# A new hand-planned order for a fused long-convolution and MLP kernel: GpSimd passes set apart from VectorE's products, diagonals on GpSimd, four row statistics on ScalarE

## The chip, the core and the metric

The kernel runs on one core of a Trainium2 chip. The time is the device time of one execution in microseconds (us); several executions are given by their median. A profile is one further execution recorded by the hardware profiler, with its own time. The engines are TensorE (PE in the profile; its weight loads are the row PEld), VectorE (DVE), ScalarE (ACT), GpSimd (POOL) and SyncE (SP), which here issues all DMAs on one queue.

## The reference, cut to what matters

All arrays are bfloat16; the sequence has 2048 rows, the width D is 512, the MLP's inner width 1792.

```python
x = A_q
h = x + A(layernorm(x), A_k, A_v, A_shift_k, A_ssm_k, A_ssm_D)
h2 = h + B(layernorm(h), B_w1, B_w2, B_w3, B_w4)

def A(q, k, v, shift_k, ssm_k, ssm_D):
    k_shift = sum over t in 0..3 of k_pad[:, t:t + S, :] * shift_k[:, 3 - t]
    kv = k_shift * v
    y = irfft(rfft(kv, 4096) * rfft(ssm_k, 4096))[:S]     # causal convolution per column
    return q * (y + kv * ssm_D)

def B(x, w1, w2, w3, w4):
    h = gelu(layernorm(x) @ w1)
    x1 = x + concat(quarters of h shifted by 1, -1, 2, -2 rows) @ w2
    return x1 + gelu(layernorm(x1) @ w3) @ w4
```

## The kernel before

**Two halves.** The 2048 rows are split in two sets `s` = 0 and 1 of eight blocks `b` of 128 partitions. The convolution is done as a Fourier transform by matmuls, in parts: the filter's first and second half (F0, F1) and the signal kv of either half (A0, A1). The first half needs only A0 with F0; the second needs A0 with F1 and A1 with F0.

**Tasks.** `body` first lists 784 tasks, each with a number, the engines that may do it, a function that issues its instructions, and what it depends on. The kinds that matter here:

- `Lf`, `Lk`, `Lv`, `Lq`, `Lw1` to `Lw4`: loads (L265 to L287, L569 to L572), 256 or 260 KB each, `Lv` 512 KB.
- `dg` (L295 to L310): the diagonal matrices of the four taps for column chunk `c`. On VectorE it is four `tensor_scalar` instructions (L307), on GpSimd one `affine_select` (L299).
- `K`, `KV`: the shift of k by matmuls with those diagonals (L442) and the product with v on VectorE (L450).
- `bits`, `cons`, `ttv`, `tta`, `f2v`, `f2a`, `ftv`, `fta`, then `tts`, `f2s`, `ft` on ScalarE: angle tables and their sines (L312 to L367); `tt`, `f2` (L370 to L378) finish them; `dr` adds ssm_D into the filter (L294).
- `S1`, `E1`, `X`, `S2`, `E2`: one forward transform: matmuls (L389), copy from PSUM (L257, on ScalarE or VectorE), a DMA that turns the layout (L405), matmuls (L413), copy from PSUM (L257; for F1 a folding by VectorE, L425).
- `P`: the products of two spectra, VectorE `tensor_tensor` of 128x2048 (L474), 8 for the first half (`conv(0)`) and 16 for the second; `I2`, `EV`, `XI`, `I1`: the inverse transform (L484, L257, the DMA of L495, L502).
- `Q`, `QV`, `QP`, `QN`: mean and variance of the rows of q: one `bn_stats` for each block on VectorE (L506), their variance for eight blocks at once, the power -0.5 on GpSimd (L529), the scales. `Y` normalizes one block of q into `z_t` (L608 to L613, GpSimd, ScalarE or VectorE); `H` adds the convolution (L616); `HS` and `SS` are statistics of rows (VectorE L602 and L603, or ScalarE L600).
- `uw`, `rr`, `hn`, `hb` and `ux`, `r1`, `xn`, `lb`: the two layer norms of the MLP part, for pairs of blocks (L623 to L649, L736 to L763); `hb` and `lb` write a normalized block (L653, L655).
- `LT`, `TE` and `LX`, `EX`: transposes of such a block, either on TensorE (L670) with a copy (L257), or by DMA through DRAM (L663, L665).
- `W`, `U` (L699, L703), `X2`, `S`, `R` (L722, L725, L729): the first MLP and its residual; `M`, `G` (L777, L781), `O`, `Z`, `OUT` (L790, L792, L794): the second MLP, by pairs of blocks.

**The order.** The string `ORDER` (L31 to L62) holds one word for each task: its number, the letter of the engine that does it (P TensorE, V VectorE, A ScalarE, G GpSimd, S the DMA queue), and digits for the buffers that it takes (`ps` is one of eight PSUM banks). `Plan.emit` (L79) issues the tasks in this order, so that each engine's queue holds its own words in order; between engines there are only the waits for data and for buffers, which the framework adds. The costs (`{V: 0.5, GP: 0.9}`) and the `port` marks in `add` were of use to the planner that wrote the string; nothing reads them when the kernel runs.

## Time and profile before

| | us |
|---|---|
| median of 3 runs (lowest, highest) | 215.55 (214.04, 215.84) |
| the profiled execution's own time | 213.26 |
| its span, first to last instruction | 211.6 |
| first instruction of the first product (L474) starts | 30.43 |
| first sum of the first half (`H`, L616) starts | 49.66 |
| first matmul with w1 (L699) in TensorE's queue | 61.8 |
| last product (L474) ends | 105.67 |
| last write to the output tile (L792) ends | 208.5 |

The granted TensorE clock was 1.00 throughout. In the views that follow, times count from the span's start; "windows" gives each engine's busy time in a stretch; "groups" gives instructions of one line and form with their count, their busy time, and the mean in ns; the timeline merges equal instructions that follow each other and gives in brackets the idle time ahead of them with what ended it.

### The profile page before, as it was taken

To read this page: it belongs to the slowest core of one execution; us is meant where nothing else is said; L and a number is where in the kernel's file an instruction comes from. 1 tells how busy PE (TensorE), PEld (TensorE's weight loads), DVE (VectorE), ACT (ScalarE), POOL (GpSimd) and SP (SyncE) were. 2 spreads that over 40 slices of the span, in tenths; PEclk is the share of its full clock that TensorE was granted. 3 is DMA by queue.
4 is the path that set the end of the run, shared out by engine and by line. 5 is a ranking of instruction groups with operands and counts; after the bars stand their busy time and mean duration, and the time that the engine had idled before them with its cause. 6 is when DMAs were issued, how large, how long until landed. Compare 5 with 4: busy or idle time off the path is not lost.

```text
span 211.6 us, 5040 instructions
## 1 busy us (share of the span) xinstructions
PE 195.7 (93%) x1964; PEld 116.2 (55%) x1980; DVE 144.8 (68%) x302; ACT 125.5 (59%) x206; POOL 80.1 (38%) x177
## 2 busy tenths in 40 slices
PE   6899769898889999979999999989999999999992
PEld 5454323442248546636744884645848888645450
DVE  6998999999999999999868971559972000112031
ACT  3979989787999658943751883364623565301010
POOL 7850059804888140287044683212765000000000
PEclk9999999999999999999999999999999999999999
DMA  6999895976948995000693008533146440010011
GB/s 173 313 403 397 321 325 222 256 205 237 371 169 294 332 435 147 0 28 13 89 232 92 27 22 181 98 69 82 42 107 154 102 74 0 3 50 34 16 50 50
DMA packets 30809, 32.86 MB, mean 155 GB/s; under 512 B 20545, under 2 KB 22594, under 8 KB 30530
## 3 DMA queue, kind: packets, MB, share of 16 engines
q1 hardware_dynamic: 30786, 32.55, 50.8%
q8 instruction: 15, 0.25, 0.5%
q14 instruction: 8, 0.07, 0.1%
HBM read 13.14 MB, written 4.46 MB: 83 GB/s over the span
## 4 chain that ended last, share of the span: by engine, by line
PE 59%; DVE 13%; ACT 12%; DMA 6%; issue 3%; POOL 3%; SPq 3%; DVEq 0%; ACTq 0%; POOLq 0%
PE ps L777 21%; PE ps L790 18%; ACT r_a L257 5%; PE ps L722 5%; PE ps L699 5%; PE ps L484 3%; DVE r_v L616 3%; DMA r_dg<-dhb 2%; DMA r_a<-r_a 2%; PE ps L502 2%; PE ps L413 2%; DMA r_k<-in_kt_dram 2%; DVE r_f L425 2%; DVE r_dg L307 1%; DVE r_p L474 1%
## 5 line engine op out<-in xcount | busy, mean ns | idle before, releaser
L777 PEld LDWEIGHTS <-r_k 128*128 128x128 bf16 x448 | 43.5, 98 | 7.7 <-issue 1.2
L792 DVE TENSOR_TENSOR r_v<-ps,r_v 128x512 bf16<-128x512 f32 x16 | 10.7, 686 | 42.4 <-PE ps L790 42.4
L474 DVE TENSOR_TENSOR r_p<-r_a,r_f 128x2048 bf16<-128x2048 bf16 x24 | 28.7, 1240 | 1.0 <-PE ps L484 0.6
L777 PE MATMUL ps<-r_dg,r_k 128*128 128x256 bf16 x224 | 25.6, 273 | 0.1
L257 ACT CAST r_a<-ps 128x1024 bf16<-128x1024 f32 x23 | 22.2, 1026 | 3.0 <-PE ps L413 2.8
L781 ACT ACTIVATE r_f<-ps 128x512 bf16<-128x512 f32 x14 | 7.8, 599 | 20.6 <-PE ps L777 20.6
L613 POOL TENSOR_SCALAR z_t<-r_q,qrs,qnm 128x512 f32<-128x512 bf16 x11 | 13.0, 1188 | 12.6 <-DVE r_v L616 12.0
L442 PE MATMUL ps<-r_dg,r_k 128*128 128x256 bf16 (+3 forms) x108 | 15.2, 284 | 1.6 <-ACT r_f L257 0.8
L257 ACT CAST r_vs<-ps 128x1024 bf16<-128x1024 f32 x14 | 13.7, 1032 | 4.9 <-PE ps L484 4.9
L725 DVE SCALAR_TENSOR_TENSOR r_q<-r_v,hrr,ps 128x512 bf16<-128x512 bf16 x16 | 11.4, 742 | 5.9 <-PE ps L722 3.7
L781 ACT ACTIVATE r_a<-ps 128x512 bf16<-128x512 f32 x14 | 7.8, 606 | 12.2 <-PE ps L777 12.2
L257 ACT CAST r_f<-ps 128x1024 bf16<-128x1024 f32 x14 | 13.2, 1023 | 3.0 <-PE ps L389 2.8
L442 PEld LDWEIGHTS <-r_k 128*128 128x128 bf16 x112 | 9.5, 98 | 9.5 <-issue 4.8
L484 PE MATMUL ps<-r_p,ttab 32*64 32x512 bf16 x384 | 13.3, 379 | 1.0 <-DVE r_p L474 0.8
L699 PEld LDWEIGHTS <-r_fx 128*128 128x128 bf16 x128 | 12.3, 98 | 3.2 <-DMA r_dg<-dhb 0.6
L600 ACT ACTIVATE junk<-r_v 128x512 bf16<-128x512 bf16 x14 | 8.9, 635 | 7.3 <-DVE r_v L616 7.1
L777 PE MATMUL ps<-xtx,r_k 128*128 128x256 bf16 x112 | 13.0, 273 | 0.0
L600 ACT ACTIVATE junk<-r_q 128x512 bf16<-128x512 bf16 x12 | 7.6, 630 | 9.2 <-DVE r_q L725 9.1
L777 PE MATMUL ps<-xty,r_k 128*128 128x256 bf16 x112 | 12.7, 272 | 0.0
L790 PE MATMUL ps<-w4s,r_f 128*128 128x512 bf16 x54 | 12.5, 379 | 0.1
L748 POOL TENSOR_TENSOR xrr<-xrr,mhalf 128x2 f32<-128x2 f32 x8 | 7.2, 900 | 14.2 <-DVE xrr L745 13.8
L389 PEld LDWEIGHTS <-f 128*32 128x32 bf16 x256 | 6.1, 95 | 11.3 <-issue 7.5
(183 smaller groups left out, 374.7 us busy)
## 6 DMA issues: line engine op xcount, KB each, us to landing
r_z<-r_vs SPq DMA_DIRECT2D x16, 256.0 KB, 3.9
r_k<-in_kt_dram SPq DMA_DIRECT2D x8, 260.0 KB, 4.6
r_v<-in_v_dram SPq DMA_DIRECT2D x4, 512.0 KB, 7.3
r_f<-r_f SPq DMA_DIRECT2D x8, 256.0 KB, 5.2
r_q<-in_q_dram SPq DMA_DIRECT2D x8, 256.0 KB, 5.7
r_a<-r_a SPq DMA_DIRECT2D x8, 256.0 KB, 4.2
r_f<-r_a SPq DMA_DIRECT2D x8, 256.0 KB, 4.2
r_a<-r_z SPq DMA_DIRECT2D x8, 256.0 KB, 4.1
```

The lines of the kernel that those rows point to most:

```text
L257: (act.copy if e in "AM" else on[e].tensor_copy)(o, i)
L442: nc.tensor.matmul(o[:, (d + j0) * P:(d + j1 + 1) * P], lhsT=kT[s][c][:, bb, x:x + P], rhs=diag[:, c, j0:j1 + 1, :].rearrange("p j x -> p ...
L474: on[e].tensor_tensor(out=prs[:, sl[0]:sl[0] + 2, :, :], in0=sp[a][:, kl, :, :, :], in1=gv, op=MUL)
L484: nc.tensor.matmul(ps[64 * t:64 * t + 64, bk[h], :], lhsT=ttab[32 * h:32 * h + 32, 2 * kl + t, 2 if x else xx, :], rhs=prs[32 * h:32 * h + ...
L600: act.activation(junk[:], x, ACT.Square, accum_out=sq[:, i, 1:2])
L613: on[e].tensor_scalar(out=z_t[:, sl[0], :], in0=qs, scalar1=qrs[:, i:i + 1], scalar2=qnm[:, i:i + 1], op0=MUL, op1=ADD)
L699: nc.tensor.matmul(ps[:, sl[0], j * 256:(j + 1) * 256], lhsT=w1s[:, k, m * P:(m + 1) * P], rhs=xt[:, k, :], start=(k == 0), stop=(k == DC ...
L725: vec.scalar_tensor_tensor(out=q_sb[:, s, b, :], in0=h_sb[s][:, b, :], scalar=hrr[:, 4 * s + b // 2, 0, b % 2:b % 2 + 1], in1=ps[:, got((" ...
L777: nc.tensor.matmul(ps[:, sl[0], j * 256:(j + 1) * 256], lhsT=w3s[:, k, fc * P:(fc + 1) * P], rhs=xt[:, k, :], start=(k == 0), stop=(k == D ...
L781: act.activation(gb[:, 2 * fp:2 * fp + 2, :], ps[:, got(("M", s, p, fp))[0], :].rearrange("p (j x) -> p j x", j=2), ACT.Gelu_apprx_tanh)
L790: nc.tensor.matmul(ps[:, sl[0], :], lhsT=gb[:, fc, (b % 2) * P:(b % 2 + 1) * P], rhs=w4s[:, fc, :], start=(fc == 0), stop=(fc == FC - 1))
L792: add(("Z", s, b), {V: 0.61}, lambda e, sl, b=b: vec.tensor_tensor(out=h_sb[s][:, b, :], in0=ps[:, got(("O", s, b))[0], :], in1=h_sb[s][:, ...
```

## The change

The statements are these; the string `ORDER` is replaced as a whole (30 lines), of which the first lines and the last one are shown.

```diff
 ORDER = """
-004S 029P0 000S 002S 003S 005S 008S 031V 037V 001S 030P 063P23 006S 055P45 009S 057P67 064V 007S 056A 038G 065P01 010S 058A 019S 059P45 033V 045G
-061P23 060A 087P60 039G 036V 062A 095P71 046V 042V 066A 093P4 032G 043V 047A 074S 101P5 044A 034G 015S 094V 051P23 022S 088V 053P01 035G 023S 052A
...
-747A 750P0 699S 753P2 751V 752S 754V 755S
+002S 029P0 000S 005S 004S 003S 008S 031V 037V 006S 030P 055P23 021S 057P45 007S 033G 056V 010S 058A 001S 038G 095P10 009S 023S 063P67 042V 059P45 015S
+036G 064A 061P23 022S 034G 101P0 060A 043V 045V 065P67 062A 046V 039V 087P41 019S 047A 044A 097P5 035G 040V 066A 102V 099P2 041A 073S 096V 032G 091P3
...
+699S 781P6 695V 696S 782V 783S
 """
...
     def dg(c):
         def f(e, sl):
-            if e == GP:
-                tap = r_k[:, c * KW + NB * 129:(c + 1) * KW].rearrange("p (j x) -> p j x", x=2)[:, :, 1:2]
-                pool.affine_select(out=diag[:, c], in_=tap.to_broadcast([P, 4, P]), compare_op=OP.is_equal, fill=0.0, base=0,
-                                   pattern=[[0, 4], [-1, P]], channel_multiplier=1)
-                return
-            for j in range(4):
-                sc = r_k[:, c * KW + NB * 129:(c + 1) * KW].rearrange("p (o x) -> p o x", o=1)[:, 0, :].bitcast(F32)[:, j:j + 1]
-                if e == A:
-                    act.activation(diag[:, c, j, :], ident[:], ACT.Copy, scale=sc)
-                else:
-                    vec.tensor_scalar(out=diag[:, c, j, :], in0=ident[:], scalar1=sc, scalar2=None, op0=MUL)
+            tap = r_k[:, c * KW + NB * 129:(c + 1) * KW].rearrange("p (j x) -> p j x", x=2)[:, :, 1:2]
+            pool.affine_select(out=diag[:, c], in_=tap.to_broadcast([P, 4, P]), compare_op=OP.is_equal, fill=0.0, base=0,
+                               pattern=[[0, 4], [-1, P]], channel_multiplier=1)
         return f
     for c in range(DC):
-        add(("dg", c), {V: 0.8, A: 1.19, GP: 0.85}, dg(c), [("Lk", 0, c)], port="VG")
+        add(("dg", c), {GP: 0.65}, dg(c), [("Lk", 0, c)], port="VG")
...
     def qstat(s, b):
-        return lambda e, sl: vec.bn_stats(qst[:, 8 * s + b, :], q_sb[:, s, b, :])
+        if s == 0 or b < 4:
+            return lambda e, sl: vec.bn_stats(qst[:, 8 * s + b, :], q_sb[:, s, b, :])
+
+        def f(e, sl):
+            act.activation(junk[:], q_sb[:, s, b, :], ACT.Identity, accum_out=qst[:, 8 * s + b, 0:1])
+            act.activation(junk[:], q_sb[:, s, b, :], ACT.Square, accum_out=qst[:, 8 * s + b, 1:2])
+        return f
...
+            if s:
+                j = slice(12, 16)
+                en.tensor_scalar(out=qmv[:, j, 0], in0=qst[:, j, 0], scalar1=1.0 / D, scalar2=0.0, op0=MUL, op1=ADD)
+                en.tensor_tensor(out=qrs[:, j], in0=qmv[:, j, 0], in1=qst[:, j, 0], op=MUL)
+                en.tensor_tensor(out=qsd[:, j], in0=qst[:, j, 1], in1=qrs[:, j], op=SUB)
+                i = slice(8, 16)
...
-            add(("Q", s, b), {V: 0.6}, qstat(s, b), [("Lq", s, b // 2)])
+            add(("Q", s, b), {A: 1.3} if s and b > 3 else {V: 0.6}, qstat(s, b), [("Lq", s, b // 2)])
```

The four statistics on ScalarE are those of blocks 4 to 7 of the second half: two activations with an accumulator each, in place of one `bn_stats`. With the new string these tasks change their engine (tasks of one kind, before and after):

| kind | VectorE | ScalarE | GpSimd |
|---|---|---|---|
| dg | 2, 0 | | 2, 4 |
| Q | 16, 12 | 0, 4 | |
| ftv, f2v | 0, 2 | | 2, 0 |
| E1, E2, EV (copies) | 22, 21 | 58, 59 | |
| HS, SS | 6, 9 | 26, 23 | |
| TE, EX (copies) | 5, 5 | 9, 9 | |
| Y | 4, 2 | 1, 3 | 11, 11 |
| hb, lb | 7, 9 | 6, 8 | 19, 15 |
| uw, ux | 7, 8 | | 9, 8 |
| hn, xn | 9, 9 | | 7, 7 |

TensorE's tasks and the DMAs are the same in number and size; their order is new. In the DMA queue the loads of v come later in the front end (`Lv` as tenth and twelfth transfer, before as ninth and eleventh), the loads of q for the first half earlier, and three of the second half's loads (`Lf` 1,0 and 1,1 and `Lk` 1,1), which stood ahead of the last two transfers `X` of A0, come behind them. On TensorE the first down projections `O` (0,3) and `O` (0,2) come ahead of the inverse transform `I2` (1,1), the last `I1` comes behind five of the next up projections, and the second half's last four pairs run in the order 0, 1, 2, 3 (before 1, 2, 0 and 3).

More of the change, by code (lines that the diff above doesn't have):

```diff
@@ new lines @@
+616G 580A 256V 569P7 617G 576A 618G3 513V 573P2 570A 275V01 414A 260P0145 577P6 509V 572A 505V 574A 578A 584P7 261V 621G2 516A 587V 277V23 619P61
+622P3 585V 588G 581P2 620A 623A 586S 589V 497V 262A 590G0 279V45 592S 591G1 281V67 273S 276P01672 278P 287V01 280P 282P 593S 289V23 624P30 284A 630P4
+291V45 283A 286S 626P5 625A 285S 582V 631A 632P6 293V67 288P01230 633A 290P 416A 299V01 292P 294P 301V23 628P4 295A 636P7 303V45 296A 634P6 627A 298S
+305V67 629A 583S 300P01231 637A 297S 302P 410V 635A 322G 304P 412V 306P 418V 638P5 307A 419G 308A 309S 310S 420V 594S2 430V1 641P4 421G3 427V0 501V
```

52 lines of the change are left out of this document (24 added, 28 removed).

## The prediction

> **What bounds the kernel now.** I read the page's busy times first, then windows cut at the milestones of the table above, then groups by form, and last the timeline where engines hand over.
>
> ```profile
> span 211.6 us, 5040 instructions
> PE 195.7 (93%) x1964; PEld 116.2 (55%) x1980; DVE 144.8 (68%) x302; ACT 125.5 (59%) x206; POOL 80.1 (38%) x177
> ```
>
> ```profile
> core 0: us, PE busy (x) PEld busy (x) DVE busy (x) ACT busy (x) POOL busy (x), PEclk, DMA share, GB/s
> 0.00:30.40 30.40, 25.36 (x317) 13.91 (x328) 27.19 (x62) 24.92 (x29) 13.23 (x69) 1.00 0.91 320
> 30.40:49.60 19.20, 16.57 (x272) 6.95 (x261) 18.18 (x18) 16.01 (x17) 10.70 (x8) 1.00 0.80 246
> 49.60:61.80 12.20, 10.87 (x135) 3.42 (x134) 11.81 (x33) 11.25 (x21) 10.03 (x20) 1.00 0.66 247
> 61.80:107.50 45.70, 44.01 (x600) 28.20 (x601) 44.49 (x72) 32.15 (x57) 18.84 (x34) 1.00 0.55 175
> 107.50:158.70 51.20, 50.01 (x332) 30.88 (x324) 36.54 (x110) 26.04 (x55) 24.31 (x43) 1.00 0.41 90
> 158.70:211.60 52.90, 48.92 (x336) 32.86 (x336) 6.61 (x11) 15.17 (x28) 2.97 (x5) 1.00 0.21 53
> ```
>
> The averages hide two kernels. Up to 61.8 us VectorE is nearly never idle (27.19 of 30.40, 18.18 of 19.20, 11.81 of 12.20), the DMA engines are 0.91 busy at first, and TensorE loses 61.8 - 25.36 - 16.57 - 10.87 = 9.0 us outright. From 61.8 on TensorE sets the end: it idles 1.69 and 1.19 us in the next two stretches, and the last one is its own work but for the final sum and output. Its work there is the same after the change. So the time can fall by as much as the front end reaches that point earlier, and by the idle 2.9 us.
>
> **The change, part by part.** The sum is made against the profiled execution, 213.26 us with a span of 211.6; it lies 2.29 below the median of 215.55.
>
> ```profile
> L474 DVE TENSOR_TENSOR r_p<-r_a,r_f 128x2048 bf16<-128x2048 bf16 x24 | 28.7, 1240 | 1.0 <-PE ps L484 0.6
> L257 DVE CAST r_a<-ps 128x1024 bf16<-128x1024 f32 x9 | 10.8, 1214 | 0.4 <-PE ps L389 0.3
> L450 DVE TENSOR_TENSOR r_kv<-ps,r_v 128x512 bf16<-128x512 f32 x16 | 10.2, 679 | 0.0
> L307 DVE TENSOR_SCALAR r_dg<-ident,r_k 128x128 bf16<-128x128 bf16 x8 | 3.1, 466 | 0.5 <-DMA r_k<-in_kt_dram 0.5
> L299 POOL TENSOR_SCALAR_AFFINE_SELECT r_dg<-r_k 128x512 bf16<-128x512 bf16 x2 | 1.3, 636 | 1.8 <-DMA r_k<-in_kt_dram 1.8
> ```
>
> ```profile
> L365 DVE TENSOR_SCALAR r_a<-r_a 128x64 int32<-128x64 int32 x1 | 0.7, 651 | 0.0
> L357 DVE TENSOR_SCALAR r_a<-r_a 128x512 int32<-128x512 int32 x1 | 0.4, 427 | 0.0
> ```
>
> *1, up to the first product (30.43 us).* VectorE loses the eight instructions of L307, 3.1 us together, and one product with v (0.68 with its place behind the first product). It gains the table passes `ftv` and `f2v`: two of 128x512 integers at 0.43 (L357) and two of 128x32, at 0.2 each between nothing and L365's 0.65: 1.3. Net 3.1 + 0.7 - 1.3 = 2.5 off its queue. GpSimd gains two diagonals at 0.64 and loses as much or more; `cons` now waits behind the first diagonal, and so for a load, which puts the tables back by up to that diagonal's 0.64, beside copies on ScalarE that hide it. The transfers are the other limit: of those ahead of the first product's spectrum none goes away, while 3 of 256 or 260 KB leave the queue ahead of A0's last (0.78 MB at the 320 GB/s of the first window: 2.4 us, which counts in step 2). So the gain is from 0 (transfers decide) to 2.5 (VectorE decides). I take 1.7, nearer to VectorE, whose first stretch is 0.89 busy with chains on it besides.
>
> *2, first product to first sum `H` (30.43 to 49.66).* Counted in the two orders, VectorE has one 1.21 copy less and one 0.68 product with v more: -0.5. Its idle 19.20 - 18.18 = 1.0 there is made of short waits for spectra and inverse transforms, all of which start earlier now. GpSimd's `Y` pass hits the products:
>
> ```profile
> L613 POOL TENSOR_SCALAR z_t<-r_q,qrs,qnm x11: 767/773/3726, 34.3 to 115.5; 128x512 f32<-128x512 bf16 x11
> ```
>
> ```profile
> 39.54 2.89 DVE L474 TENSOR_TENSOR r_p<-r_a,r_f 128x2048 bf16<-128x2048 bf16 x2
> ```
>
> One `Y` took 3.73 instead of 0.77, under products back to back; and this pair of products took 2.89 where 2 x 1.24 = 2.48 is usual, 0.4 lost. In the new order all four `Y` are planned behind the eighth product. Gain 0.5 to 1.9; I take 1.2. Floor below nothing: four `Y` that each cost a product 0.4 make it 1.6 less.
>
> *3, first sum to last product (49.66 to 105.67).* Here VectorE is the bound (11.81 + 44.49 of 57.9 busy), so its queue counts. Three `bn_stats` leave this stretch, and hb passes, copies and one resid; statistics of rows, three transposes' copies and norms come in. Counted task by task at the groups' means the two queues differ by 0.1 us: nothing. The other `bn_stats` stood behind the last product, and what hides them is TensorE's two down projections there (it is 1.69 idle in the whole stretch): nothing either, and at most 0.7 if that cover were gone. The three added small operations of `QV` lie in the same place.
>
> *4, TensorE from 61.8 to 107.5.* Two waits go, one comes.
>
> ```profile
> 87.14 1.93 PE L484 MATMUL ps<-r_p,ttab 32*64 32x512 bf16 x64
> 89.01 3.19 PE L790 MATMUL ps<-w4s,r_v 128*128 128x512 bf16 x13
> 92.59 0.40 PE L670 MATMUL ps<-ident,nbx 128*128 128x128 bf16 x4 [0.39 <-ACT nbx L653]
> 93.69 0.40 PE L670 MATMUL ps<-ident,nbx 128*128 128x128 bf16 x4 [0.71 <-POOL nbx L655]
> ```
>
> ```profile
> 86.95 0.64 ACT L600 ACTIVATE junk<-r_q 128x512 bf16<-128x512 bf16 x1
> 87.72 0.63 ACT L600 ACTIVATE junk<-r_q 128x512 bf16<-128x512 bf16 x1
> ```
>
> The transposes `LX` (0,0), (0,1) waited 0.39 and 0.71 for their input; now a down projection of 3 us stands ahead of both: -1.1. But the inverse transform of 1.93 us that stood between the seventh up projection and the first down projection is gone from there, and on ScalarE the statistic of block 4 (two passes, 87.72 - 86.95 = 0.77 apart: 1.5 us) now stands ahead of the last three gelus that the down projection needs. Queued behind that wait: both `LX`, the second down projection, then `I2` (1,1); VectorE's `Z` (0,3) and the products behind it wait with it. I take +1.4; from 0 (ScalarE is ahead) to 3.0 (a second statistic shortly before it counts too).
>
> *5, from 107.5 on.*
>
> ```profile
> L699 PEld LDWEIGHTS <-r_fx 128*128 128x128 bf16 x128 | 12.3, 98 | 3.2 <-DMA r_dg<-dhb 0.6
> ```
>
> ```profile
> 130.83 4.84 DMA r_dg<-dhb
> 135.71 4.49 PE ps L699 x32
> 207.82 0.69 DVE r_v L792
> ```
>
> TensorE idles 1.19 here, 0.6 of it ahead of 135.71 for a transpose by DMA (pair 1 of the second half) that was issued second at 130.83; it is now issued first. Late next is the transpose for pair 2, issued behind six writes: I give back 0.3 and take -0.9 (-1.2 to +1). All later work is TensorE's, instruction for instruction the same, with the same end (`O`, `Z`, `OUT`): nothing.
>
> Sum: -1.7 - 1.2 + 0 + 1.4 - 1.1 - 0.9 = -3.5. Profiled 213.3 becomes 209.8; the median, 215.55 - 3.5 = **212.0 us**. The likeliest case's own range, with the terms' spreads not all to one side, is 209.9 to 214.1.
>
> **Rivals.**
>
> *Transfers decide the front end.* Step 1 gives nothing: -1.8, **213.8**. For it the DMA share of 0.91; against it that VectorE was as busy, and did not wait.
>
> *The change does not keep them apart.* `ORDER` sets each queue's own order; as built, no `Y` of the first half waits for a product, only for its scales, which were ready when the first `Y` began at 34.3, amid products. Where GpSimd gets in between two products, each costs 0.4, four 1.6, and step 2's gain is gone: -3.5 + 1.2 + 0.4 = -1.9, **213.7**. For it the 2.89 above; against it that one `Y` in four did so before.
>
> *Table passes and diagonals collide.* L365, with 64 elements, took 0.65, as long as the diagonal beside it on GpSimd, and L307's 128x128 took 0.47. Three diagonals at 0.64 among the table passes put VectorE's chain back by up to 1.9, part of which the wait for v's load hides; 1.3 of it on the path makes -3.5 + 1.3 = -2.2, **213.4**. [...]
>
> *ScalarE becomes the bound (slower).*
>
> ```profile
> L653 ACT ACTIVATE r_k<-r_v,hnm,hrr 128x512 bf16<-128x512 bf16 x2 | 1.6, 814 | 0.9 <-DVE hnm L641 0.9
> ```
>
> Eight statistics passes (6.2), three more hb (2.4) and two more `Y` (1.6) come to it, one copy more (0.9), while three row statistics and one lb go (3.1): about +8.0 us, much of it in 49.6 to 61.8 where it is already 11.25 of 12.20 busy. Without step 4's wait the change gains 4.9. The kernel is no faster once 4.9 of the 8.0 fall on TensorE's path, slower by over 1% from 7.1; all of it: 215.55 - 4.9 + 8.0 = **218.7**. Against it: 13.5 us of ScalarE are free between 61.8 and 107.5.
>
> *Everything fits.* Steps 1 and 2 at their best, no new wait: -2.5 - 1.9 - 1.1 - 0.9 = -6.4, **209.2**.
>
> **How the numbers follow.** Forecast 0.45; transfers 0.12; not apart 0.10; collisions 0.08; ScalarE 0.17; all fits 0.08. About 1% (2.2 us) is what a measurement can tell from no change. Below 213.4: four fifths of the forecast (0.36), all of the last (0.08), and about 0.4 of the three weak cases (0.12): 0.56. Above 217.7: three quarters of ScalarE (0.13) and 0.07 for several small losses together: 0.20. Within: 0.24. The range takes in every case but the worst of ScalarE: 208.8 to 217.6.
>
> **What would show it.** Step 1: first product near 28.7 instead of 30.43, no L307. Step 2: first `H` near 46.8, no product over 1.3. Step 3: last product near 102.8. Step 4: a TensorE wait of about 1.4 for ScalarE's gelu ahead of the first down projection, none at the first `LX` pair. Step 5: the last four pairs start about 3.5 us earlier. Wrong if the first product stands at 30 or later, if TensorE's waits for ScalarE sum to 3 or more between 60 and 107, or if the tail has idle TensorE.

## The result, and the profile after

The change made the kernel slower. The median is 217.91 us over 21 runs (215.09 to 220.01) against 214.42 us over 21 runs of the kernel before (213.13 to 215.84). The ratio is 1.0105, with a 95% interval from 1.0077 to 1.0132; it leaves out runs over 1.5% above the fastest of their kernel, so it is smaller than the ratio of the medians. In microseconds the loss is 2.3 by the ratio and 3.5 by the medians; the forecast was a gain of 3.5.

The profiled execution after took 217.91 us, as long as its median. These are the head of its page, and its windows cut at the same events as those of before: first product, first sum `H`, the up projection `W` (0,0,0), the start of the two down projections behind the last products, and the end of the third pair of down projections.

```profile
span 215.9 us, 5091 instructions
PE 197.5 (92%) x1964; PEld 115.9 (54%) x1980; DVE 143.8 (67%) x299; ACT 132.8 (62%) x221; POOL 79.2 (37%) x177
...
PEclk9999965899999999999999999999999999999999
```

```profile
0.00:32.10 32.10, 25.65 (x312) 12.91 (x320) 25.73 (x56) 23.63 (x28) 12.61 (x66) 0.95 0.91 314
32.10:54.10 22.00, 19.51 (x285) 7.77 (x282) 17.87 (x18) 18.54 (x20) 12.87 (x10) 0.84 0.70 187
54.10:66.60 12.50, 10.22 (x130) 3.98 (x124) 12.38 (x31) 11.99 (x22) 10.24 (x28) 1.00 0.76 245
66.60:112.20 45.60, 43.39 (x605) 27.27 (x606) 43.49 (x74) 35.98 (x69) 18.60 (x26) 1.00 0.54 183
112.20:162.20 50.00, 48.99 (x330) 30.72 (x320) 34.63 (x104) 25.89 (x53) 21.12 (x43) 1.00 0.40 87
162.20:215.90 53.70, 49.78 (x340) 33.28 (x340) 9.66 (x19) 16.74 (x31) 3.77 (x7) 1.00 0.21 54
```

Two things are new. VectorE has less to do in the first two windows, as planned (25.73 and 17.87 us, before 27.19 and 18.18), and yet the first ends 1.7 us later and the second lasts 2.8 us longer. And the granted TensorE clock, 1.00 throughout before, is 0.95 and 0.84 there: the page's clock row drops in its sixth to eighth slice. What stands ahead of the drop is a wait of TensorE. First the waits of its weight loads for DMAs in the kernel after, from 14 to 50 us, with what ended them, their sum, count and the longest in us (line numbers of the kernel after are up to 8 lower or 4 higher than before); then TensorE's timeline, with start and duration:

```profile
PEld L405 <- DMA r_f<-r_f: 2.9, 1, 2.9
PEld L405 <- DMA r_a<-r_a: 2.7, 4, 1.1
```

```profile
24.56 1.03 PE L434 MATMUL ps<-r_dg,r_k 128*128 128x512 bf16 x7 [0.17 <-ACT r_f L257]
28.28 0.63 PE L405 MATMUL ps<-r_f,ftab 64*32 64x512 bf16 x16 [2.69 <-DMA r_f<-r_f]
```

TensorE stood still from 25.6 to 28.28 for a transpose of F0 (`X`, block group 1, 0). In the DMA queue that transpose stands behind the last load of q and the last load of v, which the new order issues ahead of it:

```profile
18.73 0.58 SPq L266 DMA_DIRECT2D r_q<-in_q_dram  x1
19.36 0.45 SPq L266 DMA_DIRECT2D r_v<-in_v_dram  x1
19.85 1.18 SPq L397 DMA_DIRECT2D r_f<-r_f  x2
```

The order alone doesn't set the length of this wait. Four experiments below have the same order of transfers up to there, and the same wait in their profiles was 2.7 (c2), 1.6 (c1), 1.1 (c3) and 0.5 us (e3). It was shorter where the transfers moved faster: from 20 to 24 us 211, 252, 261 and 299 GB/s, against 165 in the kernel after. Why the rate differs from execution to execution is open.

Later, between the up projection `W` (0,0,0) and the first product with w3 (`M`), two more waits for loads are new in TensorE's queue, 1.7 and 1.2 us, and one in VectorE's (waits of the kernel after, TensorE's from 66.6 to 87.2 us, then VectorE's from 76 to 88 us):

```profile
PEld L674 <- DVE r_k L659: 1.7, 1, 1.7
PEld L405 <- issue: 1.3, 5, 0.4
PEld L726 <- DMA r_fx<-in_w_dram: 1.2, 1, 1.2
```

```profile
DVE qst L499 <- DMA r_q<-in_q_dram: 1.4, 1, 1.4
```

The wait of 1.2 us is for w2, whose load now stands among A1's transposes. The wait of 1.7 us and VectorE's are one chain: the statistic of block 3 on VectorE waits for a load of q that is issued behind the 1.8 MB of w3, the norm passes stand behind that statistic in VectorE's queue, and TensorE's transposes `LX` (0,2), (0,3) wait for them.

This table cuts single executions at the same events for several kernels: start of the first product (P), then the stretches to the issue of the first inverse transform's DMA (XI), to the first `H`, to the up projection `W` (0,0,0) (W; it is the first up projection in the order before and the second in the order after), to the first product with w3 (M), to the second half's first `I1`, and from there to the end of the last down projection. The rows b1 to c3 are experiments, told below.

| | first P | P to XI | XI to H | H to W | W to M | M to I1 | I1 to end |
|---|---|---|---|---|---|---|---|
| before | 30.43 | 5.23 | 14.01 | 12.15 | 18.34 | 33.73 | 93.40 |
| after | 32.12 | 8.29 | 13.65 | 12.59 | 20.45 | 31.28 | 93.27 |
| difference | +1.69 | +3.06 | -0.36 | +0.44 | +2.11 | -2.45 | -0.13 |
| b1, before with diagonals | 31.19 | 5.46 | 13.90 | 12.15 | 18.36 | 33.68 | 93.46 |
| b2, before with statistics | 32.35 | 5.32 | 14.01 | 12.16 | 18.34 | 35.85 | 92.90 |
| e1, first repair | 31.12 | 6.87 | 13.59 | 15.95 | 20.15 | 31.25 | 92.99 |
| e3, statistics back | 30.44 | 8.44 | 13.47 | 12.59 | 22.00 | 32.39 | 93.52 |
| e6, three repairs | 31.12 | 6.69 | 13.51 | 12.60 | 18.69 | 31.63 | 93.57 |
| c1, second repair alone | 31.27 | 7.92 | 13.48 | 12.59 | 18.68 | 31.64 | 93.71 |
| c2, its weight load | 32.28 | 8.05 | 13.67 | 12.59 | 19.03 | 31.25 | 93.77 |
| c3, its transposes | 30.33 | 8.20 | 13.56 | 12.59 | 19.40 | 31.27 | 93.85 |

The differences add up to 4.36 us, the later end of the last down projection (211.65 against 207.29).

### The profile page after: what moved, and what is told of

Same layout as the page of the kernel before. It is cut to its first block, busy times and chain, and to the rows that moved or that the text cites. A ratio compares the mean times of both kernels' runs of the same rounds, so it can differ in the third digit from the quotient of the medians.

```text
span 215.9 us, 5091 instructions
## 1 busy us (share of the span) xinstructions
PE 197.5 (92%) x1964; PEld 115.9 (54%) x1980; DVE 143.8 (67%) x299; ACT 132.8 (62%) x221; POOL 79.2 (37%) x177
## 4 chain that ended last, share of the span: by engine, by line
PE 58%; DMA 16%; ACT 12%; SPq 4%; issue 4%; DVE 4%; POOL 1%; ACTq 0%; DVEq 0%; POOLq 0%
PE ps L781 20%; PE ps L794 20%; DMA r_q<-in_q_dram 5%; PE ps L476 5%; PE ps L726 3%; DMA r_fx<-in_fx_dram 3%; ACT junk L604 3%; PE ps L434 3%; DMA r_a<-r_a 3%; PE ps L405 3%; DMA r_z<-r_vs 3%; PE ps L381 2%; SPq L266 2%; DMA r_dg<-dhb 2%; ACT r_z L257 2%
## 5 line engine op out<-in xcount | busy, mean ns | idle before, releaser
L466 DVE TENSOR_TENSOR r_p<-r_a,r_f 128x2048 bf16<-128x2048 bf16 x24 | 29.3, 1269 | 0.1
L257 ACT CAST r_a<-ps 128x1024 bf16<-128x1024 f32 x25 | 24.1, 1026 | 2.4 <-PE ps L405 1.8
L617 POOL TENSOR_SCALAR z_t<-r_q,qrs,qnm 128x512 f32<-128x512 bf16 x11 | 15.5, 1415 | 11.3 <-DVE r_v L620 10.8
L434 PE MATMUL ps<-r_dg,r_k 128*128 128x256 bf16 (+3 forms) x109 | 16.5, 296 | 1.4 <-POOL r_dg L298 0.9
L257 ACT CAST r_f<-ps 128x1024 bf16<-128x1024 f32 x13 | 12.6, 1016 | 6.8 <-PE ps L381 4.1
L620 DVE SCALAR_TENSOR_TENSOR r_v<-ps,qsd,z_t 128x512 bf16<-128x512 f32 x16 | 11.3, 743 | 2.6 <-PE ps L494 2.3
L733 DVE SCALAR_TENSOR_TENSOR r_v<-r_q,hnm,r_v 128x512 bf16<-128x512 bf16 x16 | 12.7, 806 | 0.1
L794 PE MATMUL ps<-w4s,r_v 128*128 128x512 bf16 x54 | 12.5, 379 | 0.1
L794 PE MATMUL ps<-w4s,r_kv 128*128 128x512 bf16 x55 | 12.5, 379 | 0.1
L781 PE MATMUL ps<-xty,r_k 128*128 128x256 bf16 x112 | 12.6, 272 | 0.0
L794 PE MATMUL ps<-w4s,r_a 128*128 128x512 bf16 x55 | 12.2, 379 | 0.1
```

The costliest lines, as they stand in the source:

```text
L257: (act.copy if e in "AM" else on[e].tensor_copy)(o, i)
L434: nc.tensor.matmul(o[:, (d + j0) * P:(d + j1 + 1) * P], lhsT=kT[s][c][:, bb, x:x + P], rhs=diag[:, c, j0:j1 + 1, :].rearrange("p j x -> p ...
L466: on[e].tensor_tensor(out=prs[:, sl[0]:sl[0] + 2, :, :], in0=sp[a][:, kl, :, :, :], in1=gv, op=MUL)
L617: on[e].tensor_scalar(out=z_t[:, sl[0], :], in0=qs, scalar1=qrs[:, i:i + 1], scalar2=qnm[:, i:i + 1], op0=MUL, op1=ADD)
L620: vec.scalar_tensor_tensor(out=h_sb[s][:, b, :], in0=ps[:, got(("I1", s, b // 2))[b % 2], :], scalar=qsd[:, i:i + 1], in1=z_t[:, got(("Y", ...
L733: vec.scalar_tensor_tensor(out=h_sb[s][:, b, :], in0=q_sb[:, s, b, :], scalar=hnm[:, 4 * s + b // 2, 0, b % 2:b % 2 + 1], in1=h_sb[s][:, b ...
```

## The experiments

Each was timed in five rounds against the kernel before on the same chip; ratios are to that kernel. A word of `ORDER` names a task; those moved are named in words.

**e1: first repair.** `024S` is the last q load, `020S` v's last load, `074S` and `071S` are the transposes F0 (1,3) and (1,0), `329V` a statistic, `220V` a product with v.

```diff
-118A 024S 094V 211P20 020S 328V 114A 074S 107P45 212V 071S 109P01
+118A 094V 211P20 328V 114A 074S 107P45 212V 071S 024S 020S 109P01
...
-080A 329V 081P2345
+080A 081P2345
...
-120S 220V 125S 077V 076A
+120S 125S 077V 220V 329V 076A
```

> The changed kernel, with the last q load and the second half of v's load issued behind the forward transform's transposes F0 (1,3) and (1,0) instead of ahead of them (one statistic and one product with v move behind a copy, so that VectorE does not wait for them). Theory A (the order of the transfers made TensorE wait 2.9 us, and the idle time brought the clock down to 0.5 for 10 us): the wait ahead of F0's second step 0 falls from 2.9 to under 1.5, the granted clock stays at 1.00, the first product starts near 30.5 instead of 32.1, the first transfer of the inverse transform is issued near 36 instead of 40.4, and the time falls by 3 to 5 us, to the time of before or under it. Theory B (the passes moved to ScalarE and GpSimd are what costs): the wait goes, but the first transfer of the inverse transform stays within 1.5 us of where it is, and the time falls by less than 1.5.

Measured: 218.71 us, ratio 1.0178 (1.0120 to 1.0235). In its profile the wait of 2.9 was gone, the first product came at 31.12, the first XI at 37.99 and `H` 2.5 us earlier than in the kernel after: the front end moved the way that theory A said, though by less (XI was expected at 36). The time did not. All of it was lost again at the next place, where the second step of F1 waited 4.3 us and the clock fell at 59.3 (H to W 15.95 instead of 12.59, with a mean granted clock of 0.89):

```profile
PEld L405 <- issue: 4.6, 2, 4.3
```

Its transpose, F1 (0,1), was the fifth of that group in the queue, behind a load of q. "Issue" here is a wait that the view puts down to no releaser; the transpose landed at 58.72, and the step began at 58.83.

**e2: the wait kept, the clock held.** Eleven products of 128x512 are added ahead of that step's own, so more work is done than the reference needs.

```diff
         def f(e, sl):
+            if (sig, kl) == ("F0", 0):
+                for i in range(11):
+                    nc.tensor.matmul(ps[:, sl[0], :], lhsT=wup, rhs=diag[:, 0].rearrange("p j x -> p (j x)"), start=True, stop=True)
```

> The changed kernel with 11 products of 128x512 added on TensorE in the 2.9 us that it waits for F0's second step 0 (they go to the PSUM bank that this step overwrites; nothing else is moved). It parts the wait from the clock. Theory A, with the clock as the larger part: granted clock 1.00 all through, first product still near 32, but the transforms behind it at full speed, so that the first transfer of the inverse transform goes out 2 to 3 us earlier than 40.4 and the time falls by 2 to 3 us. Theory A with the late transfer alone: clock 1.00 and the time within 0.7 of the changed kernel's. Theory B: as the latter.

Measured: 220.39 us, ratio 1.0262 (1.0217 to 1.0307). The clock stayed at 1.00 in the front end, the first product stood at 32.47, and from there to XI it took 6.36 instead of 8.29 us, so that `H` came 2.0 us earlier: between these two profiles, about 1.9 us of the front end's loss was the clock (from 28.9 to 39.1 us 1.00 in e2 and 0.50 in the kernel after). Again the F1 place took it back and 2.5 us more (220.39 against 217.91 us), with a wait of 5.1 and the clock low from 58.6 for 6.8 us (0.93 on average from 49.0 to 60.2, 0.984 over the span).

**e3: statistics back on VectorE, e4: diagonals back on VectorE.** Single letters of the order (414, 415, 416 and 417 from A to V; 033 and 036 from G to V) with the old code for these tasks.

> The changed kernel with the four q statistics of the second half back on VectorE (one pass each instead of ScalarE's two, same places in the order, the old variance code). Theory A: the front end up to 60 us is untouched, so the time stays within 1 us of the changed kernel's. Theory B (ScalarE's eight passes of 0.63 are on TensorE's path): 2 us or more come back, with the first down projection earlier.

> The changed kernel with the diagonals 0 and 3 back on VectorE, as before the change, each as four 128x128 passes. Theory A: VectorE's queue grows by 3 us ahead of the first spectra, but TensorE still waits for the same transposes; the time is the same within 1 us or up to 1.5 longer. Theory B (diagonals on GpSimd put back the tables and the first products with v): the time falls by 1.5 us or more.

Measured: e3 217.76 us, 1.0149 (1.0106 to 1.0193); e4 218.60 us, 1.0157 (1.0099 to 1.0215). Neither undoes the loss: theory B falls for both. In e3's profile W to M and M to I1 are 1.6 and 1.1 us longer than after, so in the new order ScalarE's passes looked the better place there; the times (217.76 and 217.91 us) don't tell the two apart. In e4's profile the first product came at 31.90, no earlier than with the diagonals on GpSimd.

**e5 and e6: second and third repair, on top of e1.** `192S` is the transpose F1 (0,1), `196S` and `197S` are F1 (1,1) and (1,2), `028S` and `025S` q loads, `316S` the load of w2, `026S` the q load (1,1), `318S` the load of w3.

```diff
-338V 196S 172P45
+338V 196S 192S 172P45
...
-351A 197S 233P23
+351A 197S 316S 028S 025S 233P23
...
-387A1 316S 210V
+387A1 210V
...
-209V 318S 205P0123
+209V 026S 318S 205P0123
```

The last pair of lines is in e6 only; the old places of `192S`, `028S`, `025S` and `026S` fall away.

> The first experiment's kernel (last q load and v's last load behind the first forward transform's transposes), and the same done once more for the second half: the transpose F1 (0,1) directly behind F1 (1,1), the two q loads that stood among these transposes behind all of them, and the weight load w2 ahead of these q loads. Theory A, widened (each time a load from HBM stands ahead of a transpose in the one queue, TensorE waits for that transpose; mending one such place only shows the next): the second step of F1, 1, starts near 54.5 instead of 58.8, its wait of 4.3 us and the lower clock from 59.3 vanish, the first hT transpose comes near 60 instead of 63.9, and the time falls by 3 to 4 us from the first experiment's, to 214.5 to 216. Theory B (the passes moved to ScalarE and GpSimd): the wait goes, and ScalarE's queue of statistics, hb and copies between 50 and 66 keeps the first hT transpose at 62 or later; the time falls by less than 1.5.

> As the kernel beside it, and the q load (1,1) ahead of the 2 MB load of w3 instead of behind it. In the first experiment VectorE waited 1.8 us for that load with the statistic of block 3, and behind it stood the norm passes for which TensorE waited 2.2 us at the transposes LX (0,2). Theory A: both waits go, and the time falls by a further 1 to 2 us, to 212.5 to 214.5. Theory B: the wait for the load goes, another engine's takes its place, and the time is within 0.7 of the kernel beside it.

Measured: e5 215.15 us, 1.0045 (1.0016 to 1.0074); e6 215.07 us, 1.0044 (1.0017 to 1.0071). The second repair gives back 3.6 us of e1's 218.7, as theory A widened had it, and W is in its place again, 12.6 us behind `H` as in the kernel after. The third takes its wait away in the profile and nothing off the time. Both still hold e1's repair.

**b1 and b2: one part of the change alone on the kernel before.** Only letters of the order change (033 and 036 from V to G; 414 to 417 from V to A, with the new code of `qstat` and `qvar`).

> The kernel before with one part of the change: the diagonals 0 and 3 on GpSimd, everything else and the order as before. VectorE loses 3.1 us ahead of the first product. Theory A (ahead of the first product the transfers decide): the first product moves by less than 0.7 and the time by less than 0.7. The forecast's step 1: the first product comes 1 to 2 us earlier and the time falls by about as much. Theory B: GpSimd's tables come later, and the time rises by 1 or more.

> The kernel before with one part of the change: the four q statistics of blocks 4 to 7 of the second half on ScalarE (two passes each), at the same places in the order. Theory A: VectorE loses 2.8 us of work between 84 and 107, ScalarE gains 5 to 6 where it is free; the time changes by less than 1. Theory B (ScalarE's added passes hold up TensorE's gelus and copies): the time rises by 1.5 or more, with waits of TensorE for ScalarE between 84 and 107.

Measured: b1 215.12 us, 1.0030 (1.0000 to 1.0059): no gain, at most a small loss. VectorE had 2 us less to do up to the first product, which came no earlier (window of b1 up to it; VectorE is the third pair of numbers):

```profile
0.00:31.20 31.20, 25.64 (x312) 13.92 (x312) 25.03 (x55) 24.87 (x29) 15.88 (x71) 1.00 0.89 316
```

b2 217.09 us, 1.0089 (1.0056 to 1.0122): 1.9 us dearer. Here theory B holds: M to I1 is 2.1 us longer, and TensorE waits 3.0 us for `LX` (0,0), whose input is a pass of ScalarE (before, 0.9). The two passes of a statistic of q stood ahead of it on ScalarE, but not directly: they delayed the row statistic that started at 91.25, GpSimd's norm passes followed that one up to 95.8, and ScalarE itself was idle for 1.54 us before the pass (waits of TensorE in b2, then ScalarE's timeline):

```profile
PEld L682 <- ACT nbx L665: 3.0, 1, 3.0
```

```profile
89.73 0.63 ACT L510 ACTIVATE junk<-r_q 128x512 bf16<-128x512 bf16 x1
...
90.49 0.63 ACT L511 ACTIVATE junk<-r_q 128x512 bf16<-128x512 bf16 x1
...
95.81 0.81 ACT L665 ACTIVATE nbx<-r_q,xnm,xrr 128x512 bf16<-128x512 bf16 x1 [1.54 <-POOL xnm L768]
```

So the same statistics on ScalarE cost 1.9 us in the old order and nothing clear of noise in the new one.

**e7, e8, e9: fourth repair, and with it each part back.** v's last load goes behind three of A0's transposes (`120S`), the filter product that needs it (`219P`, `220V`) behind group 2's, and F0 (0,3) (`070S`) ahead of the last q load. e8 adds e3's edit, e9 adds e4's.

```diff
-071S 024S 020S 109P01
+071S 070S 024S 109P01
...
-120S 125S 077V 220V 329V
+120S 020S 125S 077V 329V
...
-016S 217P4 141V23
+016S 217P4 219P51 141V23
```

> All repairs of the order of transfers so far, and one more: the second half's last v load behind the transposes A0 (0,0), (1,1) and (0,1), as it stood before the change, and the one filter product and product with v that need it early (group 3, column 0) moved behind group 2, column 3; the transpose F0 (0,3) goes out ahead of the last q load. In the last repaired kernel TensorE still waited 2.1 us for the transpose A0 (0,0). Theory A (transfers): that wait falls below 1, the second step of A0, 0, starts near 26.7 instead of 28.4, the first product near 30 instead of 31.1, the clock falls in fewer runs, and the time falls by 1 to 2 us from 215.1, to 213 to 214, at or just below the kernel before. Theory B (what is left, +0.8 us, is the cost of the moved passes): the wait falls and the time stays within 0.7.

> The kernel beside it with the four q statistics of the second half back on VectorE, one pass each, at the same places in the order. With all transfers mended the passes can show their own price. If ScalarE's passes cost TensorE something in the new order (they cost 1.9 us in the old one), the time falls by 1 or more; if the new order hides them, it is the same within 0.7, or longer by up to 1.5 where VectorE is the bound (its four passes of 0.69 stand between 80 and 100).

> The same mended kernel with the diagonals 0 and 3 back on VectorE. In the old order moving them to GpSimd gave nothing (+0.6 us). Theory A (transfers decide the front end): the same within 0.7. Theory B (diagonals on GpSimd hold up the tables): faster by 1 or more. The forecast's step 1 (VectorE decides): slower by 1 or more.

Measured: e7 217.18 us, 1.0129 (1.0100 to 1.0157); e8 217.25 us, 1.0149 (1.0112 to 1.0186); e9 217.94 us, 1.0160 (1.0126 to 1.0195). The first product came at 29.73, as expected, and the time rose by 2 us: the 512 KB stood ahead of the next transpose, TensorE waited 3.1 us for it, and the clock fell for 6.8 us (0.984 on average over the span; waits of e7, 28 to 38 us):

```profile
PEld L405 <- DMA r_a<-r_a: 3.1, 1, 3.1
```

The expectation was wrong, the theory behind it was not: here the repair shifted the load to the next transpose, and the wait of 3.1 us stood there. e8 and e9 against e7 show again no cost of either part: their intervals overlap with e7's. In e9's profile the first product came at 31.91, 2.2 us later than in e7's; whether the diagonals on VectorE did that or the single execution, no run tells.

**b3: the mirror, on the kernel before.** Nothing but three loads moved up.

```diff
-067S 110V 111P23
+020S 012S 011S 067S 110V 111P23
```

> The kernel before with nothing changed but three loads (v's last, two of the second spectrum's input, 1 MB in all) issued ahead of the first transform's transposes F0 (0,0) and (1,0) instead of behind A0's: the mirror of the repairs. 1 MB at 390 GB/s is 2.6 us. Theory A: the second steps of F0, 0, and A0, 0, come 1 to 2 us later, the clock falls in more runs than before, and the time rises by 1 to 2.5 us. If the front end is bound by the vector engines, nothing moves by more than 0.5.

Measured: 217.01 us, 1.0142 (1.0105 to 1.0180): 2.6 us by the medians and 3.0 by the ratio, somewhat more than the 1 to 2.5 expected. The second steps of F0, 0, and A0, 0, came 3.0 and 3.4 us later (29.57, 30.27; expected 1 to 2), the first product came at 33.73, and no run kept the full clock (0.982 to 0.992 on average). The wait that ended last was not a transpose, though, but a load of k that stood behind the three (waits of b3, 20 to 34 us):

```profile
PEld L442 <- DMA r_k<-in_kt_dram: 4.2, 2, 3.4
```

**c1, c2, c3: the second repair alone, and its two halves.** c1 is the kernel after with the edit of e5 but without that of e1; c2 moves only `316S`, c3 only `192S`, `028S` and `025S`.

> The changed kernel with the repair of the second half's transposes alone (F1 (0,1) directly behind F1 (1,1), the two q loads behind all of F1's, the load of w2 ahead of them); the front end stays as changed, with its wait of 2.9 us and the low clock. It tells which of the two places costs. If the late transposes of F1 hide what the front end loses (the first repair alone brought nothing), the front end's loss is left and the time falls by 0.5 to 1.5 only; if the place at F1 is all that costs, the time falls by 2.5 or more, to that of both repairs (215.1).

> The changed kernel with one load moved: w2 (512 KB) directly behind the last transpose of F1, as the transfer queue stands idle there, instead of between the transposes of A1. It splits the repair that brought the kernel level with before. If the loads that come late behind A1's transposes (w2, and behind it the q load for which VectorE and then TensorE's transposes LX wait) are what costs: the stretch from the second up projection to the first gate product falls from 20.5 to about 18.7 us and the time by 1.3 to 2.3. If the order among F1's transposes costs: the time stays within 0.7.

> The other half of that repair: the changed kernel with F1 (0,1) directly behind F1 (1,1) and the two q loads behind all of F1's transposes; w2 stays between A1's. If the order among F1's transposes costs: the second step of F1, 1, comes 3 us earlier, the clock falls for less long, and the time falls by 1.5 to 3. If the loads behind A1's transposes are the cost: the wait goes, the stretch from the first sum to the second up projection stays at 12.6 us, since ScalarE fills it, and the time stays within 0.7.

Measured: c1 214.74 us, ratio 1.0000 (0.9973 to 1.0028); c2 215.84 us, 1.0056 (1.0028 to 1.0084); c3 215.53 us, 1.0041 (1.0009 to 1.0073). The second repair alone makes good the whole loss of 2.3 us by the ratio; its halves give back 1.05 (c2) and 1.4 us (c3), which their intervals hardly tell apart. The front end's wait, which I had held to be the cause, is still there in c1: 1.6 us in its profile, where it was 2.9 after, and P to XI is still 7.92. What c1 no longer has is the late loads between W and M (waits of c1, 65 to 85 us, against those of after above; then lines of c2, 66 to 87 us, and of c3, 64 to 85 us):

```profile
PEld L726 <- issue: 1.1, 3, 0.4
...
PEld L674 <- DVE r_k L659: 0.3, 1, 0.3
```

```profile
PEld L674 <- DVE r_k L659: 0.7, 1, 0.7
```

```profile
PEld L674 <- DVE r_k L659: 1.0, 1, 1.0
...
PEld L726 <- DMA r_fx<-in_w_dram: 0.8, 1, 0.8
```

The load of q behind that of w3 lands at 82.4 in the kernel after and at 78.8 in c1. That either half does this by emptying the queue ahead of w3 is argued, not shown. W to M falls from 20.45 to 19.03 (c2), 19.40 (c3) and 18.68 (c1). c3 fits neither of the theories put down for it: its time fell, but `H` to W stayed at 12.59. And e5 and e6, which have the front end's repair besides, are not below c1 (1.0045 and 1.0044 against 1.0000): that repair brought nothing.

**e10, e11, e12: what is left in e6.** e10 puts v's last load behind all of A0's transposes and `219P`, `220V` next to their group; e11 is e6 with the statistics back; e12 is e6 with eight added products in the 2.1 us that TensorE waits for A0 (0,0).

```diff
-122S 139V01
+122S 020S 139V01
...
-145S 221P6 151A
+145S 219P71 221P6 151A
...
-163V45 158P
+163V45 220V 158P
```

> The kernel with three repairs (215.1), and v's last load behind all of A0's transposes; the product that needs it moves to just ahead of its own group's next (group 3, column 1). One step on from the kernel that put the load between A0's transposes and then waited 3.1 us for A0 (0,2). Theory A: no transpose has that load ahead of it any more; the first product starts near 29.7, the fourth product pair follows without a wait of 3 us, the last product of the first half ends near 41, the clock falls in fewer runs, and the time is 212.5 to 214, at or below the kernel before. Theory B (what is left is the passes' own cost, or another transfer is late next): 214.5 to 216.

> The kernel with three repairs (215.1) and the four q statistics of the second half back on VectorE at the same places. In the order of before ScalarE's passes cost 1.9 us. If they cost as much in the new order, the time falls by 1.5 or more, and the repaired order beats the kernel before; if the new order places them where ScalarE is free, the time is the same within 0.7 or longer by up to 1.5.

> The kernel with three repairs (215.1) with 8 products of 128x512 added on TensorE in the 2.1 us that it waits for the transpose A0 (0,0) (into a PSUM bank that this step overwrites). It parts the clock from the wait where nothing later is late. If the lower clock is what is left of the loss (it fell in 10 of 12 runs), most runs show the full clock and the time falls by 0.5 to 1.2, to that of before; if not, the time stays within 0.4.

Measured: e10 214.34 us, 1.0006 (0.9974 to 1.0037), so no transpose behind a load any more brings the kernel level with before and not below; e11 215.75 us, 1.0075 (1.0046 to 1.0103), dearer than e6 by about as much as e3 was against after, each time within overlapping intervals; e12 216.00 us, 1.0034 (0.9998 to 1.0071), with the full clock (0.995 or more) in 7 of 12 runs instead of 2 of 12, and no gain beyond the interval. That e6 lacks the clock is thus not shown; an effect of half a microsecond would be lost in these intervals. No kernel tried beats the one before.

## Why the prediction was wrong

**Step 1 (up to the first product, forecast -1.7): 0.** The rival "transfers decide the front end" was right. The kernel after and four experiments share one front end (after, e3, c1, c2, c3): their first products stand at 30.3 to 32.3, mean 31.3. The kernel before and b2 share another: 30.43 and 32.35, mean 31.4. So the profile's +1.69 is within the spread of single executions, few as they are. The 3.1 us of VectorE for diagonals look partly like a wait: five of the eight passes took 0.24 to 0.27 us, and the three that ended together with a pass of GpSimd 0.61, 0.69 and 1.17. That taking them off VectorE buys nothing is shown in the old order by b1 (1.0030, and a first product no earlier); in the new one e4 and e9 are not clear of noise. The rival "the diagonals collide" was true and small: the four table passes that moved to VectorE took 2.0 us in the kernel after, one of them 0.86, as long as the diagonal beside it on GpSimd, where 1.3 was reckoned. The diagonals of the kernel before, up to its first product, with shortest, median and longest in ns:

```profile
L307 DVE TENSOR_SCALAR r_dg<-ident,r_k x8: 242/262/1172, 6.5 to 8.5; 128x128 bf16<-128x128 bf16 x8
```

The step failed where it put 1.7 "nearer to VectorE" because VectorE was 0.89 busy; the DMA engines' 0.91 in the same row was the better witness.

**Step 2 (first product to first `H`, forecast -1.2): +2.4 by the profiles, where it is the step that failed most.** I counted VectorE's queue. In the profile after, the path doesn't run through VectorE's products. From the issue of the first inverse transform's DMA to the first `H` it takes 13.2 to 14.0 us in all the profiles: eight transfers of 256 KB (DMA queue before, then after; `r_z<-r_vs` is XI), most of which wait for ScalarE's copy ahead of them (waits of the DMA queue, 30 to 56 us, before and after):

```profile
35.66 1.49 SPq L495 DMA_DIRECT2D r_z<-r_vs  x2
...
38.41 6.98 SPq L495 DMA_DIRECT2D r_z<-r_vs  x6
```

```profile
40.40 7.45 SPq L487 DMA_DIRECT2D r_z<-r_vs  x8
```

```profile
SPq L495 <- ACT r_vs L257: 7.8, 6, 4.0
```

```profile
SPq L487 <- ACT r_vs L257: 9.7, 7, 7.2
```

So in these orders `H` follows the first of them at a nearly fixed distance. The distance is not made of transfers alone: before, the last of the eight was issued some 9 us after the first and landed 3.6 later; after, 6.9 us after it and 5.5 later (47.30 to 52.80). That it would stay the same with faster engines is not shown. When the first one starts is set by how soon the first inverse transform follows the first product. Before, VectorE does six products in a row from 30.43, and TensorE begins the inverse transform right behind A0's third second step (VectorE's timeline, then TensorE's, before):

```profile
30.43 7.12 DVE L474 TENSOR_TENSOR r_p<-r_a,r_f 128x2048 bf16<-128x2048 bf16 x6
```

```profile
31.55 1.08 PE L413 MATMUL ps<-r_a,ftab 64*32 64x512 bf16 x16 [0.66 <-DMA r_a<-r_a]
32.56 1.43 PE L484 MATMUL ps<-r_p,ttab 32*64 32x512 bf16 x32
```

After, a copy stands between the first two products, and a filter product (`K`, the shift of k) and A0's last second step stand ahead of the inverse transform on TensorE; the copies of that last step are new ahead of the first `EV` on ScalarE (VectorE's timeline, then TensorE's, after):

```profile
32.11 1.25 DVE L466 TENSOR_TENSOR r_p<-r_a,r_f 128x2048 bf16<-128x2048 bf16 x1
33.29 1.21 DVE L257 CAST r_a<-ps 128x1024 bf16<-128x1024 f32 x1
34.42 1.21 DVE L466 TENSOR_TENSOR r_p<-r_a,r_f 128x2048 bf16<-128x2048 bf16 x1
```

```profile
34.52 1.89 PE L434 MATMUL ps<-r_dg,r_k 128*128 128x512 bf16 x7
36.34 1.05 PE L405 MATMUL ps<-r_a,ftab 64*32 64x512 bf16 x16
37.32 1.51 PE L476 MATMUL ps<-r_p,ttab 32*64 32x512 bf16 x24
```

P to XI is 5.2 to 5.5 us in three kernels with the old order and 7.9 to 8.4 in five with the new front end, on average 2.8 more. With the full clock (1.00 there in all three) it is 6.36 in e2, 6.69 in e6 and 6.87 in e1, so 1.1 to 1.6 of it is the order itself and the rest the clock, under which the filter product took 1.89 us (1.03 in the same place in e6). XI to `H` gives 0.4 back.

The rival "not apart" came true and did not decide: of the four `Y` that the order places behind the products, GpSimd ran all within them, one for 3.83 us, and of the six products from 37.12, two took 1.63 and 1.62 us instead of 1.21, 0.8 us lost. In the profile after that lies beside the XI chain; in e2, with the full clock, VectorE's products from 36.6 to 41.6 us are on the chain that ended last (the tile's row for `Y` on GpSimd, with shortest, median and longest in ns; then VectorE's timeline, both of the kernel after).

```profile
L617 POOL TENSOR_SCALAR z_t<-r_q,qrs,qnm x11: 767/776/3829, 36.3 to 120.9; 128x512 f32<-128x512 bf16 x11
```

```profile
37.12 7.73 DVE L466 TENSOR_TENSOR r_p<-r_a,r_f 128x2048 bf16<-128x2048 bf16 x6
```

**Step 3 (to the last product, forecast 0): +0.44 and +2.11 up to the first product with w3. This is the step that the timed experiments find at fault.** It put the stretch at nothing by VectorE's queue alone. VectorE's work was counted rightly; the loads were not counted at all. w2 and a load of q came late and TensorE waited 1.2 and 1.7 us for them; of the +2.11, 1.67 is idle time of TensorE. The change part of the prediction listed the queue's shifts for the first half only, and looked at none of the second half's loads. That c1, which moves only w2, two loads of q and one transpose of F1, mends the whole measured loss is the main finding.

**Step 4 (forecast -1.1 for the `LX` waits, +1.4 for a new wait behind ScalarE's statistic): about -1.3.** M to I1 is 2.45 shorter; 1.27 of it is idle time of TensorE that is gone, the rest work that stands elsewhere. The waits of `LX` (0,0), (0,1) went as forecast. The new wait did not come; the first down projection (L794) follows the products with w3 directly:

```profile
93.00 1.05 PE L781 MATMUL ps<-r_dg,r_k 128*128 128x256 bf16 x8
93.88 3.19 PE L794 MATMUL ps<-w4s,r_v 128*128 128x512 bf16 x13
96.91 0.61 PE L674 MATMUL ps<-ident,nbx 128*128 128x128 bf16 x8
```

The gelus were earlier than I reckoned, since TensorE itself came 7 us later to this point and ScalarE did not. The rival "ScalarE becomes the bound" is false for this order; in the old one ScalarE's passes did cost (b2: +1.9).

**Step 5 (forecast -0.9): -0.1.** The wait of 0.6 ahead of the up projection (1,1,1) is gone. As feared, the transpose for pair 2 is late in its place, and not by 0.3 only: TensorE is idle for 1.11 us from I1 on, 1.18 before.

```profile
139.35 1.91 PE L703 MATMUL ps<-r_dg,r_fx 128*128 128x256 bf16 x16 [0.35 <-DMA r_dg<-dhb]
```

**Sum.** For a typical execution: 0 (step 1), +2.4 (step 2), and for the rest 0.44 + 2.11 - 2.45 - 0.13 = 0; together +2.4, between the measured 2.3 and 3.5. With the late loads mended the rest becomes -1.0 (c1: 156.62 us from `H` to the end, before 157.62).

So three terms failed: step 1 put the choice at 1.7 for VectorE where it was 0, step 2 put -1.2 where the profiles show +2.4, and step 3 put this part of the DMA queue at nothing where c1's moves gave back 2.3 us. How the measured loss is shared between the last two is not settled: by the profiles it is step 2's, by c1's time step 3's.

What stays open: in its profile c1 reaches the first `H` 3.0 us later than the kernel before (0.8 of it up to the first product), and the rest gains 1.0, yet its time is the same within 0.3%; c1's profiled execution (215.38 us) was 0.6 above its median and that of the kernel before (213.26) 1.2 below, which makes up 1.8 of the 2.1 between them; one profile for each kernel can't close the rest. I first took the most conspicuous wait, 2.9 us with the clock drop behind it, for the cause; mending it alone (e1) brought nothing.

## What to carry to other kernels

Where one queue carries all DMAs, compare two orders by that queue first: for each transfer that an engine waits for, list what now stands ahead of it, up to the end of the loads and not only in the front end. Then look for a stretch that keeps its length in every order tried (here the first inverse transform's eight transfers with the copies between them) and ask what starts it; here work taken off VectorE, which feeds it, did not start it earlier. A wait mended alone says little until the next one behind it is mended as well.

## What the runs showed of the hardware

In these runs a lower granted clock stood behind waits of TensorE whose longest was 1.6 us (c1), 2.7 (after), 3.1 (e7), 4.3 (e1) and 5.1 us (e2). In the kernel after, the trace's clock record puts it at 0.50 for 10.24 us, from 29.0 us on. It began right behind the wait of 2.69 us (2.9 in the weight loads) and the step of 0.63 us that followed it, and TensorE was 9.0 of 10.2 us busy while it lasted. The waits of 1.62 and 1.80 us (2.1 and 2.3 in the weight loads) between 50 and 60 us in the same execution were followed by no drop: the clock was 1.00 from 50.0 to 66.6. The length of the longest wait doesn't decide it alone: in c1 no wait of the weight loads from 20 to 50 us was longer than 1.6 us, and the clock was still 0.96 from 20 to 30 us and 0.70 from 30 to 40. What sets the start and the length of a drop, these runs don't show. The row that follows is the 10.2 us of the drop in the kernel after:

```profile
28.90:39.10 10.20, 9.00 (x123) 2.92 (x122) 9.05 (x9) 8.35 (x9) 7.60 (x15) 0.50 0.76 265
```

The kernel before has lower clocks too: of 116 of its timed runs, 48 stood at a mean clock of 0.995 or more and took 214.1 us on average, 54 near 0.99 with 214.5, and 14 at 0.985 or less with 215.6 (215.0 without the four longest). Of the 21 runs after, none kept the full clock, and 15 stood at 0.985 or less. So a run with a lower mean clock tended to be longer, by half a microsecond or more. Whether the clock itself costs that is less clear: e12 had the full clock in more runs than e6 and gained nothing beyond its interval.

In one stretch loads ran far below the rate that the share of busy DMA engines suggests. While the last loads of q and v were under way, the kernel after moved 61 GB/s in one microsecond with the engines 0.71 busy, against 380 to 414 in most other stretches from 10 to 30 us. The same stretch is slow by less in the kernels with the same order there (211 to 299 GB/s from 20 to 24 us in c2, c1, c3 and e3, against 165), and the kernel before has a slow stretch too, later (234 to 266 GB/s from 24 to 28 us). The cause is open.

```profile
21.00:22.00 1.00, 1.00 (x18) 0.33 (x10) 1.00 (x2) 1.00 (x2) 0.00 (x0) 1.00 0.71 61
22.00:24.00 2.00, 1.88 (x36) 0.90 (x37) 1.72 (x3) 1.97 (x3) 0.00 (x0) 1.00 0.88 205
```
